# Tiled matmuls gathered into longer runs, an earlier second load and a longer lead for attention, in a sliding-window attention and MLP kernel

## The chip, the cores and the metric

The kernel runs on one core of a Trainium2 chip. The metric is the device time of one execution in microseconds. Times are medians of several runs; a profile is one execution, and its span (first to last instruction) stands about 1.7 us below the time of the same run.

Terms: in lines of the profile PE is TensorE's matmuls, PEld its weight loads, DVE VectorE, ACT ScalarE and POOL GpSimd, and L453 is line 453 of the kernel. The granted clock is the share of TensorE's full clock that its throttle let through. A load lands when its semaphore tells that all of it is there. PSUM is the memory, in banks, that TensorE writes to. A token block is 128 tokens. A filler is a matmul whose result nobody reads.

## The reference

Attention over 4 batches, 8 heads, 768 tokens of 64 values, where a query sees the first 4 tokens (sinks) and the last 128; then layer normalisation and a ReLU MLP (512 to 2048 to 512) with a residual.

```
scores = q @ k.T / 8;  keep = (key < 4) | (0 <= query - key < 128)
a = softmax(where(keep, scores, -1e9));  x = (a @ v), heads side by side     # [4, 768, 512]
xn = (x - mean) / sqrt(var + 1e-6) * g_ln
out = x + relu(xn @ w_ch1) @ w_ch2
```

## The kernel before

The program is a list of operations with keys. A planner written in the kernel issues them engine by engine, each at the earliest moment its own cost table allows, the smallest key first. So an edit of a key or a buffer reorders the whole program. What matters here:

```python
LEAD = 12.0                                   # how far attention runs ahead of the MLP
ps_w: 2 buffers of two PSUM banks; ps_t: one bank; ps_m: 3 banks
# in emit(): fillers on TensorE, to keep its clock, wherever the plan has it idle in the first 26 us
for _ in range(n):
    self.spin()
...
# loads of batch 0, all through GpSimd's queue, which casts to bf16
for half in range(2):
    for x in range(2):
        load_qk(0, 0, x, 4 * half, 4 * half + 4, -500 + half)   # tokens 0-383
for r in range(2):
    load_v(0, r, -490 + r)
for x in range(2):
    load_qk(0, 1, x, 0, H, -487 + 2 * x)                        # tokens 384-767: "second chunk"
...
# transposes of q or k: 12 per operation, each 128x64 (column tiles), into the single bank of ps_t
nc.tensor.transpose(pb.t[64 * h2:64 * (h2 + 1), ...], qn[(b, x)].t[:, c, 2 * hp + h2, ...], ident)
...
# scores of four heads: 64 rows each (row tiles); 4 matmuls per operation, two operations per token block
nc.tensor.matmul(pb.t[:, h2, i, 0:n], lhsT=kb.t[64 * h2:64 * (h2 + 1), 1, hp, ...],
                 rhs=kb.t[64 * h2:64 * (h2 + 1), 0, hp, ...], ...)
...
# MLP: full-array matmuls, up (256 or 512 wide) and down (512 wide), 896 in all: the bulk
```

The softmax here doesn't subtract the row's maximum and nothing guards it: scores larger than these inputs give would overflow.

## Time and profile before

| | before |
|---|---|
| time, median (lowest to highest) | 248.71 us (248.64 to 249.96), 4 runs |
| span of the profiled run | 246.9 us, mean granted clock 0.998 |
| first up-projection starts | 26.54 us |
| from there to the last matmul ("the stream") | 216.05 us |
| from the last matmul to the end | 4.34 us |
| changes of tile shape in TensorE's order | 137, of them 111 in the stream |

"The stream": from the start of the first up-projection to 0.216 us after the start of the last matmul. With start and tail it makes up the span.

The prediction below shows the main lines. From the timeline of TensorE near the end (start, length, engine, line, operation, tiles, count, idle time before and who ended it), and the busy times of 150 to 200 us (PE, PEld, DVE, ACT, POOL, then clock, DMA share, GB/s):

```profile
197.79 0.40 PE L453 MATMUL pw<-qkt 64*128 64x128 bf16 x8
199.07 1.24 PE L604 MATMUL pm<-xnt,w1s 128*128 128x512 bf16 x4 [0.89 <-DVE xnt L584]
...
150.00:200.00 50.00, 48.49 (x368) 23.25 (x374) 26.44 (x49) 22.75 (x31) 8.83 (x13) 1.00 0.12 43
```

An up-projection waits 0.89 us for the last transposed tile of its group: attention was not far enough ahead. Part of the missing 1.5 us of the stretch is only missing matmul records: the page counts 2079 matmuls to 2105 weight loads.

### The profile page before, as it was taken

The page shows a single profiled execution, that of the slowest core. Times are in us where ns is not written, and L with a number is a line of the kernel's source. Part 1 is how long each engine was busy: PE and PEld are TensorE (multiplying, and loading weights), DVE is VectorE, ACT ScalarE, POOL GpSimd, SP SyncE. Part 2 cuts the span into 40 slices and gives each one's busy share as a digit, 9 for nine tenths or more (in the row PEclk, how much of TensorE's full clock was granted, in tenths as well). Part 3 has the DMA queues.
Part 4 walks back from the last instruction along what each step waited for, and adds up shares of the span by engine and source line. Part 5 has one row for each costly group of instructions (what it writes and reads, how often), then busy time and mean ns, then how long its engine had stood idle before and what let it go on. Part 6 is the DMA issues. An engine that isn't in the chain of part 4 may idle for free.

```text
span 246.9 us, 4898 instructions
## 1 busy us (share of the span) xinstructions
PE 234.7 (95%) x2079; PEld 132.0 (53%) x2105; DVE 113.1 (46%) x222; ACT 124.5 (50%) x198; POOL 69.3 (28%) x103
## 2 busy tenths in 40 slices
PE   8887999999999999999999999999999989999993
PEld 7564778874345455444445455444444444544851
DVE  0256695020799655363752636545642630262102
ACT  2575678886550267752356753257750366400720
POOL 8984077500870844001400101101101240010000
PEclk9999999999999999999999999999999999999999
DMA  7999999999392399401210001110001210011202
GB/s 72 161 188 197 200 200 184 179 182 150 64 157 85 47 234 161 31 0 42 79 51 0 3 0 45 44 56 33 0 0 45 85 42 3 0 42 45 85 0 85
DMA packets 43621, 20.23 MB, mean 82 GB/s; under 512 B 30288, under 2 KB 40528, under 8 KB 43600
## 3 DMA queue, kind: packets, MB, share of 16 engines
q0 software_dynamic: 39616, 13.63, 48.8%
q1 hardware_dynamic: 3456, 6.29, 6.9%
q8 instruction: 16, 0.26, 0.4%
q10 hardware_dynamic: 528, 0.00, 0.1%
q14 instruction: 5, 0.04, 0.0%
HBM read 27.27 MB, written 6.29 MB: 136 GB/s over the span
## 4 chain that ended last, share of the span: by engine, by line
PE 93%; DVE 3%; ACT 2%; issue 1%; DVEq 0%; ACTq 0%
PE pm L635 34%; PE pm L604 34%; PE pw L453 5%; PE bank L360 5%; PE bank L176 4%; PE pw L512 2%; PE bank L581 2%; PE pw L515 2%; PE pw L448 2%; PE pw L505 2%; ACT qkt L166 1%; DVE ot L648 1%; PE pm L360 1%; DVE xnt L584 1%; PE pm L419 1%
## 5 line engine op out<-in xcount | busy, mean ns | idle before, releaser
L604 PE MATMUL pm<-xnt,w1s 128*128 128x256 bf16 (+1 forms) x502 | 90.2, 325 | 1.7 <-DVE xnt L584 0.9
L460 ACT ACTIVATE e<-pw 128x1024 bf16<-128x1024 f32 (+1 forms) x48 | 44.8, 952 | 39.9 <-PE pw L453 34.2
L604 PEld LDWEIGHTS <-w1s 128*128 128x128 bf16 x512 | 47.5, 98 | 32.0 <-issue 3.0
L635 PE MATMUL pm<-w2s,h1t 128*128 128x512 bf16 x247 | 59.8, 380 | 0.8 <-issue 0.5
L613 ACT ACTIVATE h1t<-pm 128x512 bf16<-128x512 f32 x61 | 36.4, 597 | 22.7 <-PE pm L604 22.3
L472 POOL TENSOR_SCALAR_AFFINE_SELECT e<-e 128x512 bf16<-128x512 bf16 x17 | 11.1, 653 | 100.3 <-ACT e L460 87.4
L635 PEld LDWEIGHTS <-h1t 128*128 128x128 bf16 x256 | 23.0, 98 | 25.9 <-issue 2.1
L613 ACT ACTIVATE h1n<-pm 128x256 bf16<-128x256 f32 x59 | 22.4, 384 | 21.4 <-PE pm L604 19.0
L648 DVE SCALAR_TENSOR_TENSOR ot<-pm,rs,xt 128x512 f32<-128x512 f32 x24 | 18.0, 749 | 30.7 <-PE pm L635 30.4
L635 PE MATMUL pm<-w2s,h1n 128*128 128x512 bf16 x121 | 30.0, 380 | 0.4 <-issue 0.2
L537 DVE RECIPROCAL rc<-pw 128x8 f32<-128x8 f32 x24 | 4.8, 201 | 48.4 <-PE pw L515 43.4
L166 ACT COPY qkt<-bank 128x768 bf16<-128x768 bf16 x22 | 17.6, 798 | 17.7 <-PE bank L360 17.4
L289 POOL DMA_DIRECT2D vn<-in_v_dram x24 | 21.5, 908 | 2.7 <-PE pw L515 2.7
L584 DVE TENSOR_TENSOR xnt<-bank,gt 128x512 bf16<-128x512 bf16 x24 | 16.5, 686 | 9.0 <-PE bank L581 8.9
L635 PEld LDWEIGHTS <-h1n 128*128 128x128 bf16 x128 | 11.3, 98 | 12.3 <-issue 1.3
L539 DVE TENSOR_TENSOR xt<-pw,rc 128x512 bf16<-128x512 f32 x24 | 16.6, 691 | 0.8
L453 PE MATMUL pw<-qkt 64*128 64x256 bf16 (+1 forms) x192 | 16.6, 265 | 0.1
L545 DVE BATCH_NORM_STATS2 st<-xt 128x6 f32<-128x512 bf16 x24 | 16.5, 689 | 0.4
L360 PEld LDWEIGHTS <-qkn 128*64 128x64 bf16 x384 | 12.1, 111 | 8.0 <-issue 7.4
L512 PE MATMUL pw<-vn,e 128*128 128x65 bf16 x192 | 15.8, 193 | 0.1
L512 PEld LDWEIGHTS <-e 128*128 128x128 bf16 x192 | 13.8, 97 | 2.3
L360 PE MATMUL bank<-ident,qkn 128*64 128x128 bf16 x336 | 14.7, 222 | 0.2 <-DVE qkt L168 0.2
(54 smaller groups left out, 181.8 us busy)
## 6 DMA issues: line engine op xcount, KB each, us to landing
out_dram<-ot SPq DMA_DIRECT2D x24, 256.0 KB, 2.0
vn<-in_v_dram POOLq DMA_DIRECT2D x24, 128.0 KB, 8.0
qkn<-in_q_dram POOLq DMA_DIRECT2D x3, 768.0 KB, 8.4
qkn<-in_k_dram POOLq DMA_DIRECT2D x3, 768.0 KB, 13.3
w1s<-in_moe_w_ch_dram POOLq DMA_DIRECT2D x4, 512.0 KB, 11.5
w2s<-in_moe_w_ch_dram POOLq DMA_DIRECT2D x4, 512.0 KB, 14.0
qkn<-in_q_dram POOLq DMA_DIRECT2D x2, 192.0 KB, 4.2
qkn<-in_k_dram POOLq DMA_DIRECT2D x2, 192.0 KB, 4.3
```

Source lines behind the costliest of these rows:

```text
L166: nc.scalar.copy(dst, src)
L289: nc.gpsimd.dma_start(vn_buf[b % 2][:, r, :, 0:D], v[b, :, 128 * r:128 * (r + 1), :].rearrange("h p d -> p h d"))
L360: nc.tensor.transpose(pb.t[64 * h2:64 * (h2 + 1), i * w + 128 * r:i * w + 128 * (r + 1)], qn[(b, x)].t[:, c, 2 * hp + h2, D * r:D * (r + 1 ...
L453: nc.tensor.matmul(pb.t[:, h2, i, 0:n], lhsT=kb.t[64 * h2:64 * (h2 + 1), 1, hp, 128 * r:128 * (r + 1)], rhs=kb.t[64 * h2:64 * (h2 + 1), 0, ...
L460: nc.scalar.activation(eb.t[:, :, :, 0:n], pb.t[:, :, :, 0:n], AF.Exp, scale=scale)
L512: nc.tensor.matmul(pv[:, half, hh, :], lhsT=ebuf[(t, half)].t[:, h2, i, 0:128], rhs=vn[:, r, h, 0:D + 1], start=fresh and hh == 0, stop=(r ...
L539: nc.vector.tensor_tensor(xb[t].t.rearrange("p (a h) d -> p a h d", a=2), pv[:, :, :, 0:D], rc[0].unsqueeze(3).to_broadcast([128, 2, 4, D] ...
L584: nc.vector.tensor_tensor(xtb[g].t[:, :, 128 * ti:128 * (ti + 1)], pt.t[:, 0:512].rearrange("p (j c) -> p j c", j=NDM), gt.unsqueeze(2).to ...
L604: nc.tensor.matmul(pb.t[:, 0:n], lhsT=w1s[:, j, 128 * ht:128 * (ht + 1)], rhs=xtb[g].t[:, j, 0:n], start=(j == 0), stop=(j == NDM - 1))
L613: nc.scalar.activation(hb.t[:, 0:n], pb.t[:, 0:n], AF.Relu)
L635: nc.tensor.matmul(pb.t, lhsT=h1b[(g, ht)].t[:, 128 * ti:128 * (ti + 1)], rhs=w2s[:, ht, :], start=(ht == 0), stop=(ht == NH1 - 1))
L648: nc.vector.scalar_tensor_tensor(ob.t, in0=pb.t, scalar=rsb[g][:, ti:ti + 1], in1=xb[t].t.rearrange("p h d -> p (h d)"), op0=ALU.mult, op1 ...
```

## The change

Its intent: fewer changes of TensorE's tile shape, an earlier start, and attention far enough ahead. The core of the diff (cut: bookkeeping of buffers, the planner's rule that holds other users of the two-bank pool back when an operation wants both its buffers, and the masks, built with one GpSimd pass less):

```diff
-                for _ in range(n):
+                for _ in range(n if s < 7.0 else n // 2):
                     self.spin()
-    LEAD = 12.0
+    LEAD = 24.0
+    W2_FIRST = 3                     # w2's last quarter is loaded behind batch 1's q and k
     for r in range(2):
-        load_v(0, r, -490 + r)
+        load_v(0, r, -486 + r)
     for x in range(2):
-        load_qk(0, 1, x, 0, H, -487 + 2 * x)
+        load_qk(0, 1, x, 0, H, -491 + x)
-        for hp in range(HP):
-            for x in range(2):
-                prep(b, 0, hp, (x,), k0 - 12 + 3 * hp + 1.5 * x, ("pt", 1))
+        for hp in range(HP):
+            prep(b, 0, hp, k0 - 12 + 3 * hp)          # q and k: 24 transposes, two-bank pool
-        scores(t, 0, key)
-        scores(t, 1, key)
+        scores(t, (0, 1), key)                        # 8 matmuls in one run
```

More of the change, by code (lines that the diff above doesn't have):

```diff
@@ L43 @@
     WARM = 26.0
+    AHEAD = 2.5
     def __init__(self, spin):
@@ L57, in ready @@
         def ready(o):
-            r = 0.0
+            r, held = 0.0, False
             for d in o.deps:
                 if d.end is None:
-                    return None
+                    return None, False
                 r = max(r, d.end)
+            n = {}
             for b in o.alloc:
                 h = hist.get(b.pool, [])
-                if len(h) >= b.bufs:
-                    for u in h[-b.bufs].users:
-                        if u.end is None:
-                            return None
-                        r = max(r, u.end)
-            return r
+                k = n[b.pool] = n.get(b.pool, -1) + 1
+                if len(h) + k >= b.bufs:
+                    for u in h[k - b.bufs].users:
+                        if u.end is not None:
+                            r = max(r, u.end)
+                        elif b.pool == "pw":
+                            held = True
+                        else:
+                            return None, False
+            return (None if held else r), held
         trace = []
@@ L74, in emit @@
             cand, first = [], {}
+            at, pairs = {}, []
             for o in waiting:
-                r = ready(o)
+                at[o], held = ready(o)
+                if (held or at[o] is not None) and sum(b.pool == "pw" for b in o.alloc) == 2:
+                    pairs.append((o.key, 0.0 if held else at[o] - self.AHEAD))
+            for o in waiting:
+                r = at[o]
                 if r is None:
+                    continue
+                if any(b.pool == "pw" for b in o.alloc) and any(o.key > k and max(r, free.get("PE", 0.0)) > a for k, a in pairs):
                     continue
@@ L225, in const_masks @@
                                 pattern=[[-1, 128]], channel_multiplier=1)
-        nc.gpsimd.affine_select(out=mask0, in_=mask1, compare_op=ALU.is_ge, fill=1.0, base=-NS,
-                                pattern=[[0, 256]], channel_multiplier=1)
     def const_negs(_):
-        for m, n in ((mask0, neg0), (mask1, neg1)):
-            nc.vector.tensor_scalar(n, m, 30000.0, -30000.0, op0=ALU.mult, op1=ALU.add)
+        nc.vector.tensor_scalar(neg1, mask1, 30000.0, -30000.0, op0=ALU.mult, op1=ALU.add)
+        for m1, m0, keep in ((neg1, neg0, 0.0), (mask1, mask0, 1.0)):
+            nc.vector.tensor_copy(m0, m1)
+            nc.vector.memset(m0[0:NS, :], keep)
     def const_sinks(_):
@@ L253 @@
     ident_done = op({"POOL": 0.35}, const_ident, [begun], -499.5)
-    masks_done = op({"POOL": 1.1}, const_masks, [begun], -488)
-    neg_done = op({"DVE": 0.5}, const_negs, [masks_done], -495)
+    half_masks = op({"POOL": 0.7}, const_masks, [begun], -488)
+    masks_done = neg_done = op({"DVE": 0.8}, const_negs, [half_masks], -495)
     sinks_done = op({"POOL": 1.4}, const_sinks, [begun], -440)
@@ L327 @@
         wi = load_w(1, c, [wi], w_key[c])
-    for c in range(4):
+    for c in range(W2_FIRST):
         wi = load_w(2, c, [wi, w_in.get((1, c))], -440 + c)
     for x in range(2):
-        load_qk(1, 0, x, 0, H, -436 + x, [wi, w_in[(2, x)]])
+        wi = load_qk(1, 0, x, 0, H, -436 + x, [wi, w_in[(1, 2 + x)]])
+    for c in range(W2_FIRST, 4):
+        wi = load_w(2, c, [wi, w_in[(2, 0)]], -434 + c)
     for r in range(RB):
@@ L336, with prep @@
     prepped, kqb = {}, {}
-    def prep(b, c, hp, what, key, pool):
+    def prep(b, c, hp, key):
         n = chunks_of[b]
@@ L347, in prep @@
         kb = kqb[b]
-        pb = Buf(*pool)
+        pb = Buf("pm", 3) if n > 1 else Buf("pw", 2)
         def go(_):
@@ L352, in go @@
                 kb.t = qkt.tile([128, 2, HP, S], BF16, name="qkt")
-            if pool[0] == "pt":
-                pb.t = pt_view
-            else:
-                pb.t = ps_m.tile([128, 512], FP32, name="pm").bitcast(BF16)
-            for i, x in enumerate(what):
+            if n > 1:
+                pb.t = ps_m.tile([128, 512], FP32, name="pm").bitcast(BF16)[:, 0:2 * w]
+                pb.t = pb.t.rearrange("d (x m) -> d x m", x=2)
+            else:
+                pb.t = ps_w.tile([128, 2, 512], FP32, name="pw").rearrange("d x m -> d (x m)").bitcast(BF16)
+                pb.t = pb.t.rearrange("d (x m) -> d x m", x=2)
@@ L358, in go @@
+            for x in range(2):
                 for r in range(e):
                     for h2 in range(2):
-                        nc.tensor.transpose(
-                            pb.t[64 * h2:64 * (h2 + 1), i * w + 128 * r:i * w + 128 * (r + 1)],
-                            qn[(b, x)].t[:, c, 2 * hp + h2, D * r:D * (r + 1)], ident)
-        deps = [ident_done]
-        for x in what:
-            for h in (2 * hp, 2 * hp + 1):
-                deps.append(loaded[(b, c, x, h)])
-        o = op({"PE": 0.06 * e * len(what)}, go, deps, key, alloc + [pb],
-               [kb] + [qn[(b, x)] for x in what])
@@ L370, in back @@
-        def back(eng):
-            nx, x0 = len(what), what[0]
-            copy(eng, kb.t[:, x0:x0 + nx, hp, c * w:(c + 1) * w].rearrange("d x (p r) -> d x p r", r=e),
-                 pb.t[:, 0:nx * w].rearrange("d (x r p) -> d x p r", x=nx, r=e))
-        n = len(what) * w
-        o = op({"DVE": 0.18 + n * 0.00101, "ACT": 0.16 + n * 0.00084}, back, [o], key, (), [pb, kb])
-        for x in what:
-            prepped[(b, c, hp, x)] = o
+                        nc.tensor.transpose(pb.t[64 * h2:64 * (h2 + 1), x, 128 * r:128 * (r + 1)],
+                                            qn[(b, x)].t[:, c, 2 * hp + h2, D * r:D * (r + 1)], ident)
@@ new lines, in prep, with back @@
+        deps = [ident_done] + [loaded[(b, c, x, h)] for x in range(2) for h in (2 * hp, 2 * hp + 1)]
+        o0 = op({"PE": 0.12 * e + 0.2}, go, deps, key, alloc + [pb], [kb] + [qn[(b, x)] for x in range(2)])
+        for xs in ([(0, 1)] if n > 1 else [(0,), (1,)]):
+            def back(eng, x0=xs[0], x1=xs[-1] + 1):
+                copy(eng, kb.t[:, x0:x1, hp, c * w:(c + 1) * w].rearrange("d x (p r) -> d x p r", r=e),
+                     pb.t[:, x0:x1, 0:w].rearrange("d x (r p) -> d x p r", r=e))
+            m = len(xs) * w
+            o = op({"DVE": 0.18 + m * 0.00101, "ACT": 0.16 + m * 0.00084}, back, [o0], key, (), [pb, kb])
+            for x in xs:
+                prepped[(b, c, hp, x)] = o
@@ L432, with scores @@
     ebuf, edone = {}, {}
-    def scores(t, half, key):
+    def scores(t, halves, key):
         b, r = divmod(t, RB)
         kb = kqb[b]
-        n = 256 if r < RB - 1 else 128
-        pb, eb = Buf("pw", 2), Buf("e", 8)
-        ebuf[(t, half)] = eb
+        last = r == RB - 1
+        n = 128 if last else 256
+        parts = [halves] if last else [(half,) for half in halves]
+        pbs, ebs = [Buf("pw", 2) for _ in parts], [Buf("e", 8) for _ in parts]
+        for eb, part in zip(ebs, parts):
+            for half in part:
+                ebuf[(t, half)] = eb
@@ L441, in scores @@
         added = t < NEG_TILES
         def mm(_):
-            pb.t = ps_w.tile([128, 2, 512], FP32, name="pw").rearrange("p a (i c) -> p a i c", i=2)
-            if added:
-                neg = (neg1 if r else neg0)[:, 0:n].unsqueeze(1).to_broadcast([128, 2, n])
-                for h2 in range(2):
-                    nc.tensor.matmul(pb.t[:, h2, :, 0:n], lhsT=ident, rhs=neg,
-                                     start=True, stop=False, skip_group_check=True)
-            for i in range(2):
-                for h2 in range(2):
-                    hp = 2 * half + i
-                    nc.tensor.matmul(pb.t[:, h2, i, 0:n],
-                                     lhsT=kb.t[64 * h2:64 * (h2 + 1), 1, hp, 128 * r:128 * (r + 1)],
-                                     rhs=kb.t[64 * h2:64 * (h2 + 1), 0, hp, 128 * r:128 * r + n],
-                                     start=not added, stop=True, skip_group_check=True)
@@ L458, in ex @@
-        def ex(_):
-            eb.t = epool.tile([128, 2, 2, 256], BF16, name="e")
-            nc.scalar.activation(eb.t[:, :, :, 0:n], pb.t[:, :, :, 0:n], AF.Exp, scale=scale)
-        def first(_):
-            ev = eb.t.rearrange("p a i c -> p (a i) c")
-            nc.vector.tensor_tensor(ev, ev, mask0.unsqueeze(1).to_broadcast([128, 4, 256]), op=ALU.mult)
-        def window(e):
-            ev = eb.t.rearrange("p a i c -> p (a i) c")
-            if e == "DVE":
-                nc.vector.tensor_tensor(ev[:, :, 0:n], ev[:, :, 0:n],
-                                        mask1[:, 0:n].unsqueeze(1).to_broadcast([128, 4, n]), op=ALU.mult)
-                return
-            nc.gpsimd.affine_select(out=ev[:, :, 0:128], in_=ev[:, :, 0:128], compare_op=ALU.is_ge,
-                                    fill=0.0, base=0, pattern=[[0, 4], [1, 128]], channel_multiplier=-1)
-            if n > 128:
-                nc.gpsimd.affine_select(out=ev[:, :, 128:256], in_=ev[:, :, 128:256], compare_op=ALU.is_gt,
-                                        fill=0.0, base=0, pattern=[[0, 4], [-1, 128]], channel_multiplier=1)
@@ L478, in scores @@
-        o = op({"PE": 0.09 + 0.23 * n / 256 + (0.43 * n / 256 if added else 0.0)}, mm,
-               ready(b, (2 * half, 2 * half + 1), 128 * r, 128 * r + n) + [neg_done], key, [pb], [kb])
-        o = op({"ACT": 0.18 + 0.84 * n / 256}, ex, [o], key, [eb], [pb])
-        if added:
-            edone[(t, half)] = o
-        elif r == 0:
-            edone[(t, half)] = op({"DVE": 0.69}, first, [o, masks_done], key, (), [eb])
-        else:
-            edone[(t, half)] = op({"POOL": 0.64 * n / 128, "DVE": 0.13 + 0.56 * n / 256}, window, [o, masks_done], key, (), [eb])
+            for pb, eb, part in zip(pbs, ebs, parts):
+                eb.t = epool.tile([128, 2, 512 // n, n], BF16, name="e")
+                pb.t = ps_w.tile([128, 2, 512], FP32, name="pw").rearrange("p a (i c) -> p a i c", c=n)
+                if added:
+                    neg = (neg1 if r else neg0)[:, 0:n].unsqueeze(1).to_broadcast([128, 2, n])
+                    for h2 in range(2):
+                        nc.tensor.matmul(pb.t[:, h2], lhsT=ident, rhs=neg,
+                                         start=True, stop=False, skip_group_check=True)
+                for i, hp in enumerate([2 * half + i for half in part for i in range(2)]):
+                    for h2 in range(2):
+                        nc.tensor.matmul(pb.t[:, h2, i],
+                                         lhsT=kb.t[64 * h2:64 * (h2 + 1), 1, hp, 128 * r:128 * (r + 1)],
+                                         rhs=kb.t[64 * h2:64 * (h2 + 1), 0, hp, 128 * r:128 * r + n],
+                                         start=not added, stop=True, skip_group_check=True)
@@ new lines, in scores, with ex, first, window @@
+        cost = 0.2 + 0.23 * n / 256 * len(halves) + (0.43 * len(halves) if added else 0.0)
+        hps = [2 * half + i for half in halves for i in range(2)]
+        o0 = op({"PE": cost}, mm, ready(b, hps, 128 * r, 128 * r + n) + [neg_done, edone.get((t - 1, 1)) if last else None], key, pbs + ebs, [kb])
+        for pb, eb, part in zip(pbs, ebs, parts):
+            def ex(_, pb=pb, eb=eb):
+                nc.scalar.activation(eb.t, pb.t, AF.Exp, scale=scale)
+            def first(_, eb=eb):
+                ev = eb.t.rearrange("p a i c -> p (a i) c")
+                nc.vector.tensor_tensor(ev, ev, mask0.unsqueeze(1).to_broadcast([128, 4, 256]), op=ALU.mult)
+            def window(e, eb=eb):
+                ev = eb.t.rearrange("p a i c -> p (a i) c")
+                m = 1024 // n
+                if e == "DVE":
+                    nc.vector.tensor_tensor(ev, ev, mask1[:, 0:n].unsqueeze(1).to_broadcast([128, m, n]), op=ALU.mult)
+                    return
+                nc.gpsimd.affine_select(out=ev[:, :, 0:128], in_=ev[:, :, 0:128], compare_op=ALU.is_ge,
+                                        fill=0.0, base=0, pattern=[[0, m], [1, 128]], channel_multiplier=-1)
+                if n > 128:
+                    nc.gpsimd.affine_select(out=ev[:, :, 128:256], in_=ev[:, :, 128:256], compare_op=ALU.is_gt,
+                                            fill=0.0, base=0, pattern=[[0, m], [-1, 128]], channel_multiplier=1)
+            o = op({"ACT": 1.02}, ex, [o0], key, (), [eb, pb])
+            if not added:
+                if r == 0:
+                    o = op({"DVE": 0.69}, first, [o, masks_done], key, (), [eb])
+                else:
+                    o = op({"POOL": 1.28, "DVE": 0.69}, window, [o, masks_done], key, (), [eb])
+            for half in part:
+                edone[(t, half)] = o
@@ L488, with weights_of @@
+    def weights_of(t, half, i, h2, lo):
+        e = ebuf[(t, half)].t
+        return e[:, h2, i + (2 * half if t % RB == RB - 1 else 0), lo:lo + 128]
     xb, xnb, xtb, mvb, rsb, turned = {}, {}, {}, {}, {}, {}
@@ L511, in mm @@
                     h = 4 * half + hh
-                    nc.tensor.matmul(pv[:, half, hh, :], lhsT=ebuf[(t, half)].t[:, h2, i, 0:128], rhs=vn[:, r, h, 0:D + 1],
+                    nc.tensor.matmul(pv[:, half, hh, :], lhsT=weights_of(t, half, i, h2, 0), rhs=vn[:, r, h, 0:D + 1],
                                      start=fresh and hh == 0, stop=(r == 0), skip_group_check=True)
                     if r > 0:
-                        nc.tensor.matmul(pv[:, half, hh, :], lhsT=ebuf[(t - 1, half)].t[:, h2, i, 128:256],
+                        nc.tensor.matmul(pv[:, half, hh, :], lhsT=weights_of(t - 1, half, i, h2, 128),
                                          rhs=vn[:, r - 1, h, 0:D + 1], start=False, stop=True, skip_group_check=True)
@@ L667, in attention @@
             values(t, key + 1.0)
-    last_cast = None
     for b in range(B):
@@ L674 @@
                 for hp in range(HP):
-                    prep(0, c, hp, (0, 1), k0 - 40 + 10 * c + hp, ("pm", 3) if hp % 2 == 0 else ("pt", 1))
+                    prep(0, c, hp, k0 + (0.6 if c else -40) + 0.1 * hp)
                 if c == 0:
-                    scores(0, 0, k0)
-                    scores(0, 1, k0 + 0.1)
-                    scores(1, 0, k0 + 0.2)
-                    scores(1, 1, k0 + 0.3)
+                    for n in range(4):
+                        scores(n % 2, (n // 2,), k0 + 0.1 * n)
                     values(0, k0 + 0.4)
@@ L683 @@
             values(1, k0 + 0.5)
-            for r in range(2, RB):
-                attention(r, akey(r)) if r > 2 else [scores(2, i, akey(2)) for i in range(2)]
+            for half in range(2):
+                scores(2, (half,), akey(2))
+            for r in range(3, RB):
+                if r < RB - 1:
+                    for half in range(2):
+                        scores(r, (half,), akey(r))
+                else:
+                    scores(r, (0, 1), akey(r))
+                values(r - 1, akey(r) - 0.5)
+            values(RB - 1, akey(RB - 1) + 1.0)
             continue
```

## The prediction

> **What bounds the kernel now.** I read the page first, then TensorE's waits, then stretches of the span, then the timeline of TensorE in two places: one in the middle, one at the start.
>
> ```profile
> span 246.9 us, 4898 instructions
> PE 234.7 (95%) x2079; PEld 132.0 (53%) x2105; DVE 113.1 (46%) x222; ACT 124.5 (50%) x198; POOL 69.3 (28%) x103
> PE 93%; DVE 3%; ACT 2%; issue 1%; DVEq 0%; ACTq 0%
> ...
> PE pm L604 <- DVE xnt L584: 0.9, 1, 0.9
> ```
>
> TensorE is busy for 95% of the span and 93% of the chain that ended last. Among its waits outside the start the longest is 0.9 us, once (at 198 us: an up-projection waited for its last transposed tile).
>
> ```profile
> 16.00:26.50 10.50, 7.96 (x128) 5.10 (x125) 6.17 (x13) 5.51 (x7) 5.17 (x11) 1.00 1.53 194
> 26.50:36.00 9.50, 9.30 (x132) 7.13 (x129) 8.64 (x19) 6.82 (x13) 3.42 (x6) 1.00 1.23 205
> 36.00:50.00 14.00, 14.00 (x141) 12.15 (x140) 4.62 (x12) 11.82 (x30) 9.50 (x12) 1.00 1.46 181
> 50.00:100.00 50.00, 49.23 (x493) 26.52 (x498) 29.94 (x56) 26.98 (x40) 20.95 (x27) 1.00 1.12 134
> ```
>
> Columns: stretch and length, then busy time (and count) of PE, weight loads, DVE, ACT and POOL, the granted clock, DMA share, GB/s. From 26.5 us on TensorE hardly rests, at full clock. So time goes only by shortening TensorE's own stream there, or by starting that stream earlier.
>
> What its stream costs is read from starts, not from busy time. Three pieces of the timeline (start, length, engine, line, count):
>
> ```profile
> 56.92 1.90 PE L635 MATMUL pm<-w2s,h1n 128*128 128x512 bf16 x8
> 58.75 0.53 PE L360 MATMUL bank<-ident,qkn 128*64 128x128 bf16 x12
> 59.21 0.61 PE L453 MATMUL pw<-qkt 64*128 64x256 bf16 x8
> 59.75 1.04 PE L635 MATMUL pm<-w2s,h1n 128*128 128x512 bf16 x4
> ...
> 66.91 0.39 PE L453 MATMUL pw<-qkt 64*128 64x256 bf16 x4
> 67.23 0.82 PE L635 MATMUL pm<-w2s,h1n 128*128 128x512 bf16 x3
> ...
> 195.30 1.04 PE L635 MATMUL pm<-w2s,h1t 128*128 128x512 bf16 x4
> 196.27 0.39 PE L453 MATMUL pw<-qkt 64*128 64x256 bf16 x4
> 196.59 1.04 PE L635 MATMUL pm<-w2s,h1t 128*128 128x512 bf16 x4
> ```
>
> Down-projection matmuls start 0.216 us apart. Four of them ahead of a run of scores take 0.97 (195.30 to 196.27), not 0.864: 0.10 us is lost on entering the 64-row tiles. Four scores take 0.32 to the next full matmul, eight take 0.54, so four cost 0.22 and 0.10 is lost on leaving. Over all such places in the trace entry and exit are 0.095 us each. The transposes (128x64 tiles) pay the same: eight down matmuls before them take 1.83 instead of 1.73.
>
> The start is bound otherwise:
>
> ```profile
> 16.05 0.76 POOL L304 DMA_DIRECT2D w1s<-in_moe_w_ch_dram  x1 [0.76 <-DMA qkn<-in_k_dram]
> 16.07 0.53 PE L360 MATMUL pm<-ident,qkn 128*64 128x128 bf16 x12
> 17.58 0.95 DVE L168 COPY qkt<-pm 128x768 bf16<-128x768 bf16 x1
> 19.80 0.60 PE L448 MATMUL pw<-mask,ident 128*128 128x512 bf16 x2
> 22.71 0.60 PE L448 MATMUL pw<-mask,ident 128*128 128x512 bf16 x2
> 26.54 1.04 PE L604 MATMUL pm<-xnt,w1s 128*128 128x256 bf16 x8
> ```
>
> The second chunk of k was issued at 8.61 and landed 7.2 us later, at 15.8; its transposes start at 16.07, the last of them at 19.3 (one private PSUM bank is shared with the transposes of x and with the fillers), the scores of token block 2 at 19.80 and 22.71, and the up-projection only at 26.54.
>
> **What the Trainium skill says.** "TensorEngine Tiling (Array Packing)", Key Properties: changing the tiling mode drains TensorE. The trace agrees, 0.095 us per change. "TensorE: Matmul & The Clock Gate", Back-to-back issue gap: N/2.4 + 2.5 ns, 216 ns at N=512; the trace has 0.216. "Perfetto Trace Analysis", TensorE timeline: the profiler computes a matmul's end rather than observing it; hence starts are used here (one 512-wide matmul shows 0.38 us, yet the next starts after 0.216). The clock page, table "Why this matters for your kernels": no idle gaps over about 3 us between bursts, else half clock. Before, the start's fillers keep the clock at 1.00 from 6.8 us; the change drops 54 of 113 fillers, so this bears on a rival.
>
> **The change part by part.** I counted tile-shape changes in TensorE's instruction order of both built kernels.
>
> 1. Merged runs. All real matmuls keep their number and shape. Changes of tile shape fall from 137 to 96; from the first up-projection on, from 111 to 67 (scores of both halves back to back, 24 transposes in a run instead of 12). 44 x 0.095 = 4.2 us off a stream that never rests: all of it on the path.
>
> 2. The start. Rates: q's second chunk landed at 13.7 and k's at 15.8, so 2.0 us each; k's earlier piece landed at about 9.0. Now the second chunk is issued at 4.9 and 5.9 instead of 7.7 and 8.6, right behind: q at about 11.0, k at 13.0 (2.8 us earlier). v0 and v1 (0.9 each) land at 13.9 and 14.8 instead of 9.9 and 10.7.
> By hand, with the durations of the trace (copy 0.80, exp 1.02, score group with its mask matmuls 0.76 to 0.91, 0.2 from an engine's end to the next start): transposes of heads 4-7 at 9.1 (now five fillers ahead instead of 17, which ended at 9.5); all four copies on ACT, so exps start at 11.0, 12.0, 13.2, 14.5 (before 11.3 to 14.4: no gain); second-chunk transposes between 13.2 and 16.7; values 0 at 14.5, which waits for the exp and not for v; last copy on ACT 17.9; scores of block 2 at 16.7 and 18.1 (before 19.8 and 22.7); their exps end at 18.9 and 20.0; sink scores 19.4; block 3 at 20.2 and 21.2, each waiting for a PSUM buffer; values 2 at 22.2; first up-projection at 22.9. Before: 26.54. Gain 3.6 us, and by then one more score group is done (it stood after the up-projection's start before).
>
> 3. What is left after that start. Sum of nominal starts from the order, plus changes: before 202.4 + 111 x 0.095 = 212.9; after 201.8 + 67 x 0.095 = 208.1. The stream took 216.0 before (26.54 to 242.6), so 3.1 us of waits and rounding.
>
> 4. Attention ahead by 24 instead of 12, and transposes in a two-buffer pool: takes away the 0.98 us at 198 and the 0.35 us at 62.3, where a transpose waited for the copy out of the single bank. Against it, new waits just after the earlier start: block 4's scores need a PSUM buffer that DVE frees about 0.25 us late, and ACT carries exps (1.02) between evacuations of 0.38. I put waits at 3.0, nearly unchanged.
>
> 5. Masks: one POOL pass less (0.4 us), done at about 8.3 on DVE, needed at 9.7: hidden.
>
> Sum: 22.9 + 208.1 + 3.0 = 234.0 for the last matmul, plus the unchanged 4.3 us tail (last output) = 238.3 of span; measured times stood 1.8 above the span before (248.72 against 246.9). That gives 240.1; hand-built starts err early, so I say 240.6.
>
> **The rivals.** (a) Weights late. w2's last chunk now goes behind batch 1's q, k and v. Continuous loading puts it at about 53.5, and by TensorE's order it is wanted at about 54.8. For: POOL, which issues it, must first get through window masks and row statistics, and its queue waits on landings. Against: 1.3 us of slack. If it slips by 3 us TensorE stands 2 us: 242.5. (b) The start stays tied to a chain of ACT and PSUM buffers: v later by 4 us, all four copies on ACT. For: exps gain nothing by my own walk. If the up-projection begins at 25 the time is 242.7. (c) Clock. Fewer fillers leave gaps of about 1.5 us; if one stretch falls to half clock, 1 to 2 us are lost. Against: gaps stay under 3 us. (d) ACT or DVE becomes the bound where attention is pulled ahead: ACT is busy 11.8 of 14 us in 36 to 50. For: exps crowd. Against: from 50 on both are near half busy, and the totals don't change. If it bites, 2 us, near 242.6.
>
> **Range and chances.** Part 1 is arithmetic on measured gaps (4.2 us, sure to 0.5). The start gives 3.6 with an error of about 1.5. New waits may cost 0 to 3. Two rivals together reach 244; all going well, 238.5. Two per cent faster is 243.7. Chances: faster 0.88, within two per cent 0.11, slower 0.01.
>
> **What would show it.** TensorE's first up-projection at 22 to 24 us; the second chunk of k landed near 13; shorter TensorE time from there to the last matmul, about 211 us instead of 216, with 24 transposes or 8 scores between single entries and exits; no wait near 1 us late in the span; granted clock 1.00 after 7 us. It would be wrong if the gap between down matmuls and tiled runs did not shrink in number, if TensorE idled before the third or fourth down-projection quarter (w2), or if the first up-projection still came after 25.

## The result, and the profile after

| | before | after |
|---|---|---|
| time, median of 4 runs | 248.71 us | 242.20 us (240.94, 242.18, 242.22; one slow run at 245.29) |
| span of the profiled run | 246.93 us | 239.23 us |
| first up-projection starts | 26.54 us | 24.09 us |
| stream | 216.05 us | 210.79 us |
| last matmul to end | 4.34 us | 4.35 us |
| changes of tile shape, in all and in the stream | 137, 111 | 96, 67 |

The ratio is 0.971 (95% interval 0.966 to 0.976). It is the mean of one kernel's fast runs over that of the other's in the same rounds, so not quite the ratio of the medians. The span shrank by 7.7 us: 2.45 in the start, 5.26 in the stream. Two things to keep in mind. Not all of the stream's 5.26 is saved work: one score group (0.6 us, the difference of 202.4 and 201.8 in the prediction's third part) now stands ahead of the first up-projection, so it moved from the stream into the start. And of the start's 2.45 us, 1.35 are the earlier start of the second chunk's transposes (16.07, now 14.72), but 1.10 are a shorter way from there to the first up-projection (10.47, now 9.37 us). Which of the other edits shortened that way was not tested.

From the page of the changed kernel (its line numbers are shifted: 380 transposes, 475 scores, 542 and 545 values, 634 up, 665 down), with TensorE's first wait and the stretch late in the span:

```profile
PE 228.8 (96%) x2051; PEld 130.3 (54%) x2051; DVE 119.6 (50%) x231; ACT 121.1 (51%) x193; POOL 59.3 (25%) x86
PE 85%; DVE 6%; DMA 4%; POOL 2%; ACT 1%; issue 1%; POOLq 0%
...
PE pm L380 <- DMA qkn<-in_k_dram: 2.5, 3, 1.2
...
150.00:200.00 50.00, 50.00 (x339) 24.86 (x340) 24.74 (x44) 21.86 (x32) 3.75 (x5) 1.00 0.12 43
```

Against the lines of before: TensorE's busy share barely moved, 95 to 96%, because work and span shrank together; a reader who looks at busy shares alone sees nothing. The chain of work that ended last has 4% of DMA in it now, which it did not have: a load of k. It is also TensorE's largest wait. In 150 to 200 us TensorE never rests; the wait at 198 us is gone.

A merged run in the stream:

```profile
47.78 2.35 PE L634 MATMUL pm<-xnt,w1s 128*128 128x256 bf16 x20
50.06 0.86 PE L380 MATMUL pw<-ident,qkn 128*64 128x128 bf16 x24
50.85 1.04 PE L665 MATMUL pm<-w2s,h1n 128*128 128x512 bf16 x4
51.82 0.36 PE L380 MATMUL pw<-ident,qkn 128*64 128x128 bf16 x6
```

24 transposes take 0.79 us from start to the next start, where before 12 took 0.46. Entry and exit are paid once: the four down matmuls still take 0.97 instead of 0.864 ahead of the next tiled run.

The start:

```profile
14.72 0.36 PE L380 MATMUL pm<-ident,qkn 128*64 128x128 bf16 x6 [1.21 <-DMA qkn<-in_k_dram]
15.01 0.60 PE L471 MATMUL pw<-mask,ident 128*128 128x512 bf16 x2
15.55 0.39 PE L475 MATMUL pw<-qkt 64*128 64x256 bf16 x4
15.89 0.42 PE L542 MATMUL pw<-vn,e 128*128 128x65 bf16 x8
...
24.09 0.60 PE L634 MATMUL pm<-xnt,w1s 128*128 128x256 bf16 x4
```

TensorE waits 1.21 us for the second chunk of k, which lands at 14.68 us. The values of block 0 begin at 15.89, and v0 landed at 15.84.

Last, the runs differ by their clock. The one at 240.94 us had a mean granted clock of 1.000; those at 242.18 and 242.22 had 0.986 and 0.993.

### The profile page after: what moved, and what is told of

Same layout as the page of the kernel before. It is cut to its first block, busy times and chain, and to the rows that moved or that the text cites. A ratio compares the mean times of both kernels' runs of the same rounds, so it can differ in the third digit from the quotient of the medians.

```text
span 239.2 us, 4785 instructions
## 1 busy us (share of the span) xinstructions
PE 228.8 (96%) x2051; PEld 130.3 (54%) x2051; DVE 119.6 (50%) x231; ACT 121.1 (51%) x193; POOL 59.3 (25%) x86
## 3 DMA queue, kind: packets, MB, share of 16 engines
q0 software_dynamic: 39616, 13.63, 50.6%
## 4 chain that ended last, share of the span: by engine, by line
PE 85%; DVE 6%; DMA 4%; POOL 2%; ACT 1%; issue 1%; POOLq 0%
PE pm L665 34%; PE pm L634 34%; PE pw L475 4%; DMA qkn<-in_k_dram 4%; PE pw L380 3%; PE bank L611 3%; PE pw L542 2%; DVE xt L569 2%; POOL qkn L292 2%; PE pw L545 2%; DVE qkt L183 2%; PE pw L535 1%; ACT qkt L181 1%; DVE st L575 1%; PE pw L471 1%
## 5 line engine op out<-in xcount | busy, mean ns | idle before, releaser
L486 ACT ACTIVATE e<-pw 128x1024 bf16<-128x1024 f32 x44 | 43.7, 1023 | 49.8 <-PE pw L475 49.6
L665 PE MATMUL pm<-w2s,h1t 128*128 128x512 bf16 x256 | 58.9, 379 | 0.0
L665 PEld LDWEIGHTS <-h1t 128*128 128x128 bf16 x256 | 24.1, 98 | 28.1 <-issue 1.1
L643 ACT ACTIVATE h1n<-pm 128x256 bf16<-128x256 f32 x63 | 24.0, 384 | 18.7 <-PE pm L634 15.8
L594 POOL TENSOR_SCALAR ve<-mv 128x2 f32<-128x2 f32 (+1 forms) x8 | 2.4, 305 | 82.6 <-DVE mv L578 82.1
L183 DVE COPY qkt<-pw 128x768 bf16<-128x768 bf16 x10 | 9.6, 958 | 21.6 <-ACT qkt L181 21.2
L498 POOL TENSOR_SCALAR_AFFINE_SELECT e<-e 128x512 bf16<-128x512 bf16 (+1 forms) x8 | 6.1, 759 | 49.6 <-ACT e L486 49.6
L496 DVE TENSOR_TENSOR e<-e,mask 128x1024 bf16<-128x1024 bf16 x22 | 15.0, 687 | 5.8 <-ACT e L486 5.6
L380 PEld LDWEIGHTS <-qkn 128*64 128x64 bf16 x384 | 11.4, 109 | 8.9 <-issue 3.6
L475 PE MATMUL pw<-qkt 64*128 64x256 bf16 (+1 forms) x192 | 14.8, 263 | 0.2 <-DVE qkt L183 0.2
```

Source lines behind the costliest of these rows:

```text
L380: nc.tensor.transpose(pb.t[64 * h2:64 * (h2 + 1), x, 128 * r:128 * (r + 1)], qn[(b, x)].t[:, c, 2 * hp + h2, D * r:D * (r + 1)], ident)
L475: nc.tensor.matmul(pb.t[:, h2, i], lhsT=kb.t[64 * h2:64 * (h2 + 1), 1, hp, 128 * r:128 * (r + 1)], rhs=kb.t[64 * h2:64 * (h2 + 1), 0, hp, ...
L486: nc.scalar.activation(eb.t, pb.t, AF.Exp, scale=scale)
L643: nc.scalar.activation(hb.t[:, 0:n], pb.t[:, 0:n], AF.Relu)
L665: nc.tensor.matmul(pb.t, lhsT=h1b[(g, ht)].t[:, 128 * ti:128 * (ti + 1)], rhs=w2s[:, ht, :], start=(ht == 0), stop=(ht == NH1 - 1))
```

## The experiments

The theory: the stream shrank because 44 changes of tile shape at 0.095 us went away (4.2 us) and the wait at 198 us with them; the start came forward because the second chunk landed earlier; what is short of the forecast is the landing of that chunk and of v0. Rivals: fewer waits rather than changes of shape; the earlier start owed to other edits; fewer fillers, and so a lower clock. All experiments start from the changed kernel. First all of them in numbers, then one by one.

| run | median, us | ratio to before | first up-projection | stream | mean granted clock of the runs |
|---|---|---|---|---|---|
| changed kernel | 242.20 | 0.971 | 24.09 | 210.79 | 1.000, 0.986, 0.993 (and 0.982, slow) |
| e1_fill | 243.31 | 0.973 | 26.63 | 210.78 | 4 of 6 at 0.992 or 0.993 |
| e2_t_break | 243.73 | 0.978 | 23.85 | 213.63 | 4 of 4 at 0.996 or more |
| e3_t_edge | 243.37 | 0.975 | 24.79 | 211.55 | 4 of 4 at 0.991 to 0.993 |
| e4_c1_from_c0 | 241.17 | 0.968 | 24.39 | 210.78 | 1 of 4 at 0.993 |
| e5_v_first | 242.88 | 0.976 | 23.14 | 213.59 | 1 of 4 at 0.993 |
| e6_lead12 | 242.04 | 0.972 | 24.28 | 211.95 | 2 of 4 at 0.988 and 0.990 |
| e7_s_apart | 242.86 | 0.975 | 23.76 | 212.90 | 1 of 4 at 0.993 |
| e8_free_start | 241.84 | 0.971 | 22.03 | 213.57 | 4 of 4 at 0.998 or more |
| e9_swap | 243.51 | 0.978 | 26.58 | 210.80 | 4 of 4 at 0.992 or 0.993 |
| e10_swap_free | 239.28 | 0.961 | 22.39 | 210.79 | 4 of 4 at 0.996 or more |
| e11_fill_dma | 241.15 | 0.969 | 24.85 | 210.80 | 6 of 6 at 0.996 or more |
| e12_mixed_fill | 242.49 | 0.974 | 23.43 | 213.53 | 6 of 6 at 0.997 or more |

First up-projection and stream are those of the one profiled execution of each kernel; the 2% rule calls all of them faster than before, but e2 and e9 unclear (their intervals reach 0.982). The stream repeats to 0.02 us wherever the program behind the first up-projection is the same (six profiles at 210.78 to 210.80), while times scatter by 2 us. So what concerns the stream is read from the stream, and the scatter lies in the start.

### Is it the changes of shape? (e2_t_break, e3_t_edge)

```diff
             for x in range(2):
+                if n == 1 and x == 1:          # e2: between the 12 of q and the 12 of k
+                    nc.tensor.matmul(raw[:, 1, 0:128], lhsT=spinner, rhs=spinner, start=True, stop=True, ...)
```

e3 has `x == 0` instead: the same matmul ahead of the run. The transposes overwrite what it writes.

> The changed kernel with one dummy full-array matmul (128 wide) in the middle of each of the 12 runs of 24 transposes of batches 1 to 3: 24 more changes of tile shape. Theory (0.095 us a change): TensorE's stream from the first up-projection to the last matmul grows by 12 x 0.056 + 24 x 0.095 = 2.9 us, from 210.8 to 213.7 us, and the time by as much. Rival (the gain came from fewer waits and the earlier start, not from the changes of shape): under 1 us.

> The same 12 dummy matmuls, but ahead of each run of transposes, where TensorE changes shape anyway (only 3 more changes, where two runs stood side by side). Theory: stream longer by 12 x 0.056 + 3 x 0.095 = 1.0 us, to 211.8 us, so 1.9 to 2.0 us less than with the dummy in the middle. Rival: the dummy itself costs, and both variants take the same.

TensorE's timeline of the first such run, e2 and then e3:

```profile
49.82 0.53 PE L384 MATMUL pw<-ident,qkn 128*64 128x128 bf16 x12
50.28 0.23 PE L380 MATMUL pw<-spinner 128*128 128x128 bf16 x1
50.44 0.53 PE L384 MATMUL pw<-ident,qkn 128*64 128x128 bf16 x12
50.90 0.39 PE L669 MATMUL pm<-w2s,h1n 128*128 128x512 bf16 x1
```

```profile
50.66 0.22 PE L380 MATMUL pw<-spinner 128*128 128x128 bf16 x1
50.81 0.86 PE L384 MATMUL pw<-ident,qkn 128*64 128x128 bf16 x24
```

In e2 the run takes 50.90 - 49.82 = 1.08 us instead of 0.79. The stream grew by 2.84 us in e2 and by 0.76 in e3 (forecast 2.9 and 1.0). Both have 12 equal extra matmuls; e2 has 21 more changes of shape and is 2.08 us longer: 0.099 us each. The theory holds. The times of e3 do not show it, since all four of its runs lost clock (0.991 to 0.993; the profiled one from 11.02 us on, ahead of the stream); the stream does.

### The scores, and the lead (e7_s_apart, e6_lead12)

```diff
-        scores(t, (0, 1), key)
+        for part in ([(0, 1)] if t % RB == RB - 1 else [(0,), (1,)]):
+            scores(t, part, key)
```

> The changed kernel with the two halves' scores issued as two operations again in batches 1 to 3 (14 more changes of tile shape after the first up-projection). Theory: stream longer by 14 x 0.095 = 1.3 us, to 212.1 us, if waits stay as they are. Rival (one run of eight scores needs two free PSUM buffers at once, so apart it waits less): less than 0.7 us longer.

The stream grew by 2.11 us, more than the 1.3 of the changes. The rest is waits: new ones of 0.76 us at 76.8 us (values after a run of transposes found no free two-bank buffer) and 0.34 at 56.9 (scores, for an exp), less 0.44 and 0.21 near 85 us in the changed kernel, which went. So the run agrees with the price for scores, but is too mixed to measure it. The rival did not show: issued apart, TensorE waited more, not less, since the planner, asked differently, made a worse order.

```diff
-    LEAD = 24.0
+    LEAD = 12.0
```

> The changed kernel with attention 12 instead of 24 units ahead of the MLP. Theory (the longer lead removed the wait of an up-projection for its last transposed tile): stream from the first up-projection to the last matmul longer by 0.5 to 1.2 us than 210.8, of which 0.2 from two more changes of shape, with one wait near 1 us in the second half. Rival (merged runs removed the waits too): stream within 0.3 us of 211.0.

```profile
191.10 0.40 PE L611 MATMUL bank<-ident,xn 128*128 128x128 bf16 x4 [0.61 <-DVE xn L583]
192.28 1.02 PE L634 MATMUL pm<-xnt,w1s 128*128 128x512 bf16 x4 [0.78 <-DVE xnt L614]
```

The wait of before is back, in two pieces, and the stream is 1.16 us longer, of which 0.2 are two more changes of shape. The longer lead is worth about 1 us. The medians (242.04 against 242.20) hide it behind the clock: at 1.000 the run with the short lead took 241.70, the changed kernel 240.94.

### The clock (e1_fill)

```diff
-                for _ in range(n if s < 7.0 else n // 2):
+                for _ in range(n):
```

> The changed kernel with the halving of the fillers after 7 us taken back (75 fillers instead of 59), same order of everything else. Clock theory: three of the four runs of the changed kernel had a granted clock of 0.982 to 0.993 and took 242.2 to 245.3 us, the one at 1.000 took 240.9; if too few fillers let the clock fall at the start, every run is now at 0.997 or more and near 240.9 us. Rival (the clock record varies whatever the fillers): clocks between 0.98 and 1.00 again, median near 242.2 us.

The clock theory, in this form, falls: four of six runs lost clock again. The profiled one shows where. Busy times in two stretches of e1, clock in the third column from the right:

```profile
13.00:16.40 3.40, 1.03 (x14) 0.51 (x14) 0.27 (x1) 0.92 (x1) 1.32 (x2) 1.00 2.09 172
16.40:19.80 3.40, 3.40 (x50) 2.49 (x49) 2.46 (x5) 2.19 (x3) 3.21 (x9) 0.50 1.55 193
```

For 3.42 us the clock is half. In the stretch of the same length before it TensorE was busy for only 1.03 us, waiting for k, which in this run landed at 15.69. Half of 3.42 us in 242 is 0.7%: a mean of 0.993 fits one such fall, and one of 0.986 two. Nor is it new with the change: in the 29 runs of the kernel before that went beside these experiments, 9 had a mean clock of 0.991 or less and took about 250.1 us instead of 248.7 (none of the nine was profiled). In the changed kernel and the three variants with the same start order (e1, e2, e3) it was 11 of 18, the slow run counted. But these are not spread evenly: e2 had none in 4 runs and e3 had 4 in 4, though their starts are the same program. So runs of one build are not independent tries, or something else takes part; that stays open. The taken-back fillers (16 of the 54 that the change dropped) were put where the planner thinks TensorE idle, not where it waits for a load that is late.

### What sets the start (e4, e5, e8, e9, e10)

```diff
-    qn[(b, x)].t[:, c, 2 * hp + h2, D * r:D * (r + 1)]
+    qn[(b, x)].t[:, 0, 2 * hp + h2, D * r:D * (r + 1)]     # e4: second chunk's transposes read the first chunk
```

> Wrong result on purpose: the transposes of the second token chunk of batch 0 read the first chunk, so they do not wait for the second chunk's landing (14.7 us in the changed kernel); all loads stay. Theory (the landing of k sets the start): first up-projection earlier by about 1.2 us, 24.1 to about 22.9 us as the prediction had it, and the time about 1.2 us less. Rival (the chain of ACT copies, exps and PSUM buffers sets it): first up-projection within 0.4 us of 24.1.

```profile
16.18 0.42 PE L542 MATMUL pw<-vn,e 128*128 128x65 bf16 x8 [1.62 <-DMA vn<-in_v_dram]
```

A miss: the first up-projection came at 24.39, not earlier. (The median is 1.0 us lower, which goes with fewer runs that lost clock: the profiled run at 0.999 took 241.22, the changed kernel's at 1.000 took 240.94.) Without k's landing TensorE gets on to the values of block 0 and waits 1.62 us for v0. So v0, moved behind the second chunk by the change, binds just as k does. (The output still passed the comparison: q and k are drawn with a spread of 0.1, so the scores are near zero and swapped keys hardly show. This kernel, and e8 and e10 with the same edit, are wrong all the same.)

Where TensorE does wait for k and for no later load, k sets the start to a hundredth: in four profiles without a fall of the clock (changed kernel, e6, e7, e11) k landed anywhere from 14.36 to 15.44 us, and the first up-projection came 9.36 or 9.37 us after the start of the transposes that had waited for it.

```diff
-        load_v(0, r, -486 + r)                 # e5: the old order of loads, re-planned
+        load_v(0, r, -490 + r)
-        load_qk(0, 1, x, 0, H, -491 + x)
+        load_qk(0, 1, x, 0, H, -487 + 2 * x)
```

> The changed kernel with the old load order (v0 and v1 ahead of the second chunk of q and k). Theory (loading the second chunk earlier brought the start forward by 2.4 us): k lands near 15.8 us again, and time and last matmul are 1 to 2.4 us later than the changed kernel's (last matmul at 234.7 us). Rival, after the run whose transposes did not wait for k and gained nothing because v0 then released TensorE at 16.1: the swap only trades one landing for the other, and the last matmul is within 0.6 us of 234.7; the earlier start came from the other edits.

k landed at 16.17 and the last matmul came 1.85 us later than in the changed kernel, as the theory said. But the planner changed the whole order with it: the first up-projection came at 23.14 with 1.5 us of attention work left for later, and the stream got new waits (an up-projection 0.8, two of 0.5 for copies). The run cannot tell the start apart from the rest. e8, the same with e4's edit, says as much: 

> Wrong result on purpose: v first, and the second chunk's transposes read the first chunk, so neither landing stops TensorE at the start. Theory (landings set the start of the changed kernel, k or v0, whichever is last): last matmul at least 1 us earlier than 234.7 us, time near 239.5 us in runs at full clock. Rival (copies, exps and PSUM buffers set it): last matmul within 0.5 us of the run with v first alone.

Against e5 the last matmul came 1.13 us earlier, so landings bind there too; but the last matmul (235.39) and the time (241.84) came later than forecast, because the re-planned stream is 213.57 us long.

So the next two kept the plan and exchanged only what the load queue does in its slots (cut: the making of the two lists):

```diff
+    for i in range(2):                         # e9; e10 has e4's edit as well
+        v_ops[i].fn, qk_ops[i].fn = qk_ops[i].fn, v_ops[i].fn
```

> The changed kernel with every engine's compute in the same order, but the loads of v0, v1 and of the second chunk of q and k exchanged in the load queue (the old load order). The load order alone, nothing re-planned. Theory: v lands near 10 us, k near 15.8 to 16.2 instead of 14.7; the first up-projection, 24.1 us in the changed kernel, moves by the 1.2 to 1.5 us of k, to about 25.4, with the stream after it unchanged at 210.8. Rival (v0 was as binding as k, one only trades for the other): within 0.5 us of 24.1.

> Wrong result on purpose: as the exchange of loads, but the second chunk's transposes read the first chunk, so neither v0 nor the second chunk of k can hold TensorE; the order of compute is that of the changed kernel. Theory (the step of the prediction that failed is when those loads land, not the chain of copies, exps and buffers that was walked by hand): first up-projection at 22.5 to 23.0 us, as predicted with k at 13.0 and v0 at 13.9, and 1.1 to 1.6 us before the changed kernel's 24.1. Rival (the hand-walked chain was too short): later than 23.6 us.

The first up-projection of e10, and two stretches of e9:

```profile
22.39 0.60 PE L637 MATMUL pm<-xnt,w1s 128*128 128x256 bf16 x4
```

```profile
12.50:15.90 3.40, 0.84 (x11) 0.31 (x10) 0.00 (x0) 1.46 (x2) 2.24 (x3) 1.00 1.72 189
15.90:19.30 3.40, 3.29 (x36) 1.79 (x38) 1.59 (x3) 1.02 (x1) 2.68 (x7) 0.50 1.54 193
```

With neither v0 nor the second chunk in its way, the same order of compute reaches the first up-projection at 22.39 (forecast 22.5 to 23.0) and the kernel takes 239.28 us. The chain of copies, exps and buffers that the prediction walked by hand gave 22.9 with landings at 13.0 and 13.9, so the walk was sound to about 0.5 us and the landings were not: they cost the profiled run of the changed kernel 24.09 - 22.39 = 1.70 us, of which 0.3 already through the first chunk of k (landed at 9.39, in e10 at 9.09). In e9 k landed at 15.96, and the first up-projection came at 26.58: 2.5 us later, twice what k's 1.3 us explain. The other half is a fall of the clock after 3.4 us in which TensorE was busy for 0.84; all four runs lost as much clock (0.992 or 0.993) and agree within 0.2 us (243.43 to 243.60). So in this plan the order of loads is worth 2.5 us between these two profiled runs, half of it through the clock, and 1.3 us by the medians (243.51 against 242.20), since the changed kernel lost clock in most of its runs too. Over all profiles, k landed at 14.17 to 15.69 us in the eight with the new order of loads (mean 14.79) and at 15.76 to 16.21 in the five with the old one (16.03).

### Versions meant to be better (e11_fill_dma, e12_mixed_fill)

```diff
+            for _ in range({(0, 0, 2): 22, (0, 1, 0): 16}.get((b, c, hp), 0)):
+                spin()                         # e11: ahead of the two runs of transposes that wait for loads
```

> The changed kernel with 38 more fillers placed just where TensorE sits waiting for landings at the start (22 ahead of the transposes of heads 4 to 7, 16 ahead of the second chunk's). Theory (a stretch of waiting lets the granted clock fall for 3.4 us in about half of the runs of all these kernels): all runs at 0.997 or more, and a median near 241 us. Rival (the clock falls for another reason, or needs more than this): one third of runs or more at 0.993 or less again, median near 242.5.

The same stretch as e9's in e11, then in the profiled run of the changed kernel, whose clock held; last the stretch ahead of the fall in e3:

```profile
12.50:15.90 3.40, 1.97 (x33) 1.41 (x30) 0.02 (x1) 1.24 (x2) 1.06 (x2) 1.00 2.04 158
```

```profile
12.50:15.90 3.40, 2.19 (x25) 0.75 (x24) 0.78 (x1) 1.70 (x2) 1.64 (x2) 1.00 2.16 169
```

```profile
7.60:11.00 3.40, 1.22 (x29) 0.80 (x27) 1.04 (x4) 1.00 (x3) 3.40 (x5) 1.00 1.27 143
```

All six runs kept 0.996 or more, with a median of 241.15 us, close to what the theory said. In three profiles the clock fell after a stretch with TensorE busy for 0.84, 1.03 and (e3) 1.22 of 3.4 us; where it was 1.97 or 2.19 it held, and also where it was 1.79 (e4, 13.63 to 17.04). That fits fillers at the waits holding the clock. It is not shown beyond doubt: e2 held it in 4 of 4 runs without them. This is the best correct version that was run: 0.969 of before, against 0.971 for the changed kernel. That is 1.05 us by the medians, with overlapping intervals, and measured in different rounds; at full clock the two are alike (240.78 the fastest, against 240.94). What it gains is that none of its six runs fell.

> A version meant to beat both: second chunk loaded by half of the heads, first half ahead of v0 and v1, second half behind, with 28 more fillers at the waits. Theory: first half of k near 12.5, v0 near 14, so scores of block 2 need not wait for all of it: first up-projection about 1 us earlier than 24.1, median 240 us if the clock holds. Rival (TensorE is released by the later landing, which only changed its name): first up-projection at 24 or later.

Half right. The first half of k landed at 12.63 and the first up-projection came at 23.43, but the re-planned stream had 2.7 us of other waits (three of about 1 us between 80 and 87 us), and the time was worse than e11's. It is the lesson of e5 again: with this planner no load is moved alone.

## Why the prediction was right

It forecast 240.6 us in a range of 238.5 to 244; the median is 242.20, and the run at full clock 240.94. Of its own signs, the stream of about 211 us, the single entries and exits and the missing wait late in the span came true. The first up-projection (24.09) stood just outside 22 to 24, k did not land near 13, and the clock stayed at 1.00 in one of three fast runs only.

1. Merged runs: right, and the largest part. 44 changes less; the price per change was confirmed at 0.099 us by e2 and e3 for the transposes.
2. The start: right in direction, mis-sized. The step that failed is "q at about 11.0, k at 13.0" and "v0 and v1 (0.9 each) land at 13.9 and 14.8". They landed at 12.61, 14.68, 15.84 and 16.40. The prediction took the 3.0 us between v1 and q's second chunk before for its late issue. Issued early it still came 3.2 us after the load ahead of it. The packet records show that the bytes were not late: counted in the order of issue, k's were through at 13.1 us, just as forecast, and k landed 1.6 us later. "DMA: Bandwidth & Descriptors", Why a DMA increments its semaphore by 16 and not by 1, states that a DMA runs on up to 16 engines which finish independently and counts as landed only when all have. A last share that comes late, while other engines are already at the loads behind, would give such a lag; but the packet records here do not name the engine, so this is not shown, and the first load of q, with nothing ahead of it, lags by 0.55 us as well. In the kernel before, k's lag was 1.1 us. That it grew need not be due to the change: with the new order of loads it was 1.1 (e4), 1.25 (e2) and 2.5 us (e1), with the old one 1.5 (e9). The step "values 0 at 14.5, which waits for the exp and not for v" fell with it: v0 landed at 15.84, and the values began at 15.89. The first up-projection came at 24.09 instead of 22.9: 1.2 us. e10 shows that the rest of the walk was sound to about 0.5 us, on the long side; that this covered part of the landings' 1.7 us is luck.
3. The stream: 211.1 forecast (208.1 of work, 3.0 of waits), 210.8 measured. So its 5.26 us are 4.2 of changes of shape, 0.6 of the score group that moved ahead of it, and 0.4 fewer waits and rounding (3.1 before, 2.7 after).
4. The lead: right. The wait at 198 us went, e6 brought it back. The wait of block 4's scores for a buffer did not come: they start at 27.07, right behind an up-projection. The waits that came are others, 0.31 us at 27.78 for a normalised tile and, the longest, 0.44 at 85.21. w2's last quarter landed at 53.66 (forecast 53.5), and in the stream TensorE waited for no load: rival (a) did not happen. Rival (b) did in part, through v as it said. Rival (d) did not: TensorE rested nowhere for ACT.
5. The masks: done at 8.8, used at 10.06; hidden, as forecast.
6. The clock, rival (c), happened: by their mean clock, two of the three fast runs lost as much as one fall of 3.4 us (0.993) and two (0.986); they took 1.3 us more than the third. Neither was profiled. The prediction held against this rival that gaps stay under 3 us. They did, and the clock fell all the same in e1, e3 and e9, where TensorE had waited for loads; giving back 16 fillers elsewhere (e1) did not help.

The sum closes for the run at full clock: 240.1 of the part-by-part sum, + 1.2 of the start, - 0.3 of the stream = 241.0, against 240.94. The other 1.3 us to the median are put down to the clock, but are no more than the difference between runs: the one that lost twice as much clock (0.986, 242.18 us) took no longer than the one at 0.993 (242.22).

## What to carry to other kernels

Where TensorE never rests, count its changes of tile shape: each cost 0.095 us here, gathering small tiled matmuls into fewer runs took it away, and the gain was forecast from the instruction order alone. A load's landing could not be forecast from its bytes and its place in the queue alone (k: 14.17 to 15.69 us with one order of loads); leave a microsecond or two, and ask which other load moves back when one is moved forward. When runs of one kernel scatter in two groups, look at the clock and at the stretch just before it fell: fillers elsewhere (e1) did not help, fillers at the waits (e11) seem to have.

## What the Trainium skill lacked or had wrong

- "TensorEngine Tiling (Array Packing)", Key Properties, has the drain at a change of tiling mode but no price: here 0.095 us on entry and on exit, for 128x64 tiles (0.099 between e2 and e3) and 64x128 tiles alike.
- "TensorE: Matmul & The Clock Gate", table "Why this matters for your kernels", asks for no idle gaps over about 3 us. Here the clock fell without such a gap: in e9 the waits were 0.76 and 1.90 us with work between them. What went ahead of each of three falls was 3.4 us with TensorE busy for 0.84 to 1.22; at 1.79 (e4) it held.
- "DMA: Bandwidth & Descriptors" says that the engines of a DMA finish independently, not how far apart: here the second chunk of k landed 1.1 to 2.5 us after its bytes, counted in the order of issue, were through. How much of that is the engines' doing is not shown.
